# An attention block's backward tail: weights loaded in the last head group, partial sums in the drain, DMA transposes, modulation gradients off TensorE

## The chip, the core and the metric

One core of a Trainium2 chip runs the kernel as one launch. The core has five engines, each with its own instruction stream, in order: TensorE (PE in the profile, with its weight loads as PEld), VectorE (DVE), ScalarE (ACT), GpSimd (POOL) and SyncE (SP, which here only issues DMAs). Sixteen DMA engines move data between DRAM (HBM) and the on-chip memory (SBUF); TensorE writes into PSUM, eight banks of 512 f32 columns by 128 partitions. The engines wait for each other through semaphores. The metric is device time of one execution, in microseconds, as the median over runs.

## The reference

A transformer block with adaptive layer norm and its whole backward pass: n = 2048 tokens, width D = 512, H = 32 heads of 16, dense width 1792, everything bf16 in DRAM.

```python
mod = (silu(c) @ w_mod).reshape(1, 6, 1, 512)          # sa, ca, ga, sb, cb, gb
h = layernorm(x) * (1 + ca) + sa
x = x + ga * attention(h, wqkv, wo)
h = layernorm(x) * (1 + cb) + sb
out = x + gb * (relu(h @ w1 + b1) ** 2 @ w2 + b2)
# and the vjp with grad_out: dx, dwqkv, dwo, dw1, db1, dw2, db2, dc, dw_mod
```

Four of the gradients come last, since they need the gradients dq, dk and dv of all heads. dh1 = [dq dk dv] wqkv^T is a 2048 x 512 x 1536 product. From it the gradient of the first layer norm is formed and added to the residual's, which gives dx. dwqkv = h1^T [dq dk dv]. The six rows of modulation gradients (dsa, dca, dga, dsb, dcb, dgb, each a sum over the tokens) give dw_mod, an outer product of silu(c) with the rows, and dc = silu'(c) times (w_mod times the rows).

## The kernel before, in words

The forward pass comes first. `prep()` (to about 41 us) makes the statistics of the first layer norm, the modulation vectors and the first projections. Its DMAs are issued by SP through the helper `sp`, which has one line in the profile (L178). Among them are 16 DMA transposes of w_mod (`wmod_turn`), which make four of the six transposed blocks of w_mod and store them in DRAM as `wmT_st`. Forward attention runs over heads with ACT's exponentials (L567); chunks of the dense layer and stages of preparation (`later_stage`, one every fourth unit) are slipped between. Stages 30 and 31 transpose the other two blocks of w_mod; stage 25 takes reciprocals of two modulation rows.

The attention backward (about 1140 to 2380 us) goes over 8 head groups of four heads; in each over 4 blocks of 512 keys (kc), 4 blocks of 512 queries (qc) and 4 tiles of 128 queries in such a block (qi): 512 units. Four units make a block b, which has the same kc and qc. The order of every instruction is written by hand: two lists of tokens, `order_t` and `order_n`, are gone through in turn, one per block. A token stands for a score matmul (s, L1603), an exponential on ACT (e, L1609), a pair of dP products with dS = dP * E on VectorE (D, L1623, L1625), the quads for dk and dv (q: L1663, L1672, the accumulator accVK), the transposes of dS on PE (t, L1653, copied by ACT at T, L1769), and the quads for dq (d, L1690) with their output (Q: ACT L1703 and an addition on POOL L1708). Most transposes of dS are DMA transposes issued by SP (L1638, L1640). A dictionary `todo` holds work due after a given number of dP pairs: `at(j, f, ...)` puts it there; `load` issues a DMA from ACT. Finished dk, dv pieces go to DRAM as `dVKtP` (eight tiles of 128 rows by 2048 tokens, two of them stay in SBUF) and dq as `dQc` (four tiles). Before the last group ends, five of these whole tiles (512 KB each) are loaded back by SP (`load_grads`).

After the last exponential the loop runs three blocks longer to drain its pipeline. Then comes the part with names ending in J. SP loads the other gradients, the weights `wT_all` (12 blocks of 128 x 512, 1.5 MB), the last rows of dq from SBUF (L1793), tiles of x and of the incoming dx (`load_x`, L1802, L1804) and rows of modulation gradients that went through DRAM (`rows_st`, L1808). PE transposes all twelve gradient tiles, 16 transposes each (L1944), and VectorE and ACT copy them out of PSUM (L1950, L1952) for dwqkv. Then for each of the 16 token tiles:

- PE makes dh1 with 12 matmuls (L1884).
- VectorE multiplies by 1 + ca with a sum along the row (L1888), takes the product with the normalised x with another sum (L1891), scales both sums (L1894), subtracts (L1907) and adds the rest with the residual's gradient (L1909). ACT makes the normalised tile (L1877) and the correction tq (L1896).
- PE adds up the two products over the tokens with a column of ones (`row_sums`, L1903).
- Beside that PE turns rows into columns (L1849, pcolK), adds up the c gradient with the transposed w_mod (L1855, pdc) and makes the outer products of dw_mod (L1862, pwm), which ACT copies out (L1863).

Last come 12 chains of 16 matmuls for dwqkv (L1918), each copied out by ACT and VectorE (L1922, L1929, L1931) and stored by SP. Rows 0 and 1 of the modulation gradients, which need all 16 tiles, are worked off between these chains.

## Time and profile before

| what | us |
|---|---|
| median of three runs | 2525.15 |
| lowest and highest | 2521.43, 2525.73 |
| span of the profiled execution | 2517.6 |
| PE, ACT, DVE, POOL busy | 2342.5, 2302.3, 1810.1, 350.0 |
| last exponential of the backward ends | 2380.0 |
| first full dh1 matmul of the tail | 2406.7 |
| first dwqkv matmul | 2466.6 |
| last dwqkv matmul ends | 2513.8 |

The profiled execution has a span from its first to its last instruction; the time of an execution is somewhat longer than that. Columns of a window: us, then busy time (and count) of PE, PEld, DVE, ACT and POOL, then the granted clock of PE, the DMA engines' busy share (over 1 where their packets overlap) and GB/s. A group line gives line, engine, operation, output and input, shapes and count, then busy time and the mean ns of one, then the idle time before them and what ended it. A chain line gives start, duration, what. In a timeline line the bracket at the end is the idle time before it and its releaser.

### The profile page before, as it was taken

The page shows a single profiled execution, that of the slowest core. Times are in us where ns is not written, and L with a number is a line of the kernel's source. Part 1 is how long each engine was busy: PE and PEld are TensorE (multiplying, and loading weights), DVE is VectorE, ACT ScalarE, POOL GpSimd, SP SyncE. Part 2 cuts the span into 40 slices and gives each one's busy share as a digit, 9 for nine tenths or more (in the row PEclk, how much of TensorE's full clock was granted, in tenths as well). Part 3 has the DMA queues.
Part 4 walks back from the last instruction along what each step waited for, and adds up shares of the span by engine and source line. Part 5 has one row for each costly group of instructions (what it writes and reads, how often), then busy time and mean ns, then how long its engine had stood idle before and what let it go on. Part 6 is the DMA issues. An engine that isn't in the chain of part 4 may idle for free. (4 is left out here: it accounts for less than half of the span.)

```text
span 2517.6 us, 49897 instructions
## 1 busy us (share of the span) xinstructions
PE 2342.5 (93%) x19005; PEld 776.3 (31%) x19005; DVE 1810.1 (72%) x2341; ACT 2302.3 (91%) x3577; POOL 350.0 (14%) x379
## 2 busy tenths in 40 slices
PE   7899889989988999999999999999999999999999
PEld 3232223222322323442233322233323323322343
DVE  5556153454435454579999999999999999998862
ACT  7999999999989999539999999999999999999842
POOL 2000000211323142210111101111010111100100
PEclk9999999999999999999999999999999999998999
DMA  6476455367658766979999999999999999999972
GB/s 202 136 193 165 150 122 139 96 161 144 103 85 176 151 134 119 261 208 191 202 199 210 196 206 208 201 207 202 207 202 202 209 195 203 195 208 212 196 237 72
DMA packets 1220981, 447.15 MB, mean 178 GB/s; under 512 B 1096951, under 2 KB 1191607, under 8 KB 1220486
## 3 DMA queue, kind: packets, MB, share of 16 engines
q1 hardware_dynamic: 1192822, 409.11, 82.2%
q0 software_dynamic: 10944, 16.78, 4.8%
q10 hardware_dynamic: 16976, 18.07, 2.8%
q8 instruction: 149, 2.44, 0.4%
q14 instruction: 90, 0.74, 0.1%
HBM read 96.75 MB, written 73.95 MB: 68 GB/s over the span
## 5 line engine op out<-in xcount | busy, mean ns | idle before, releaser
L1625 DVE TENSOR_TENSOR dS_u<-psD_u,E_u 128x1024 bf16<-128x1024 f32 x1024 | 1186.0, 1218 | 71.6 <-PE psD_u L1623 24.0
L567 ACT ACTIVATE ET<-psST 128x1024 bf16<-128x1024 f32 x1024 | 942.0, 1260 | 27.0 <-PE psST L565 26.5
L1609 ACT ACTIVATE E_u<-psS_A 128x512 bf16<-128x512 f32 x768 | 513.1, 668 | 10.5 <-PE psS_C L1603 8.5
L1609 ACT ACTIVATE E_u<-psS_B 128x512 bf16<-128x512 f32 x768 | 505.8, 659 | 12.1 <-DMA dsT<-dS_u 3.0
L1623 PE MATMUL psD_u<-iv,ido 32*128 32x512 bf16 x2048 | 409.6, 388 | 0.0
L565 PE MATMUL psST<-qt_sb,kt_sb 32*128 32x512 bf16 x2048 | 317.8, 387 | 62.0 <-ACT ET L567 46.6
L1609 ACT ACTIVATE E_u<-psS_C 128x512 bf16<-128x512 f32 x512 | 335.4, 655 | 3.3 <-PE psS_B L1603 1.4
L1603 PE MATMUL psS_B<-ik,iq 32*128 32x512 bf16 x768 | 295.3, 385 | 12.8 <-ACT E_u L1609 5.5
L1603 PE MATMUL psS_A<-ik,iq 32*128 32x512 bf16 x768 | 293.4, 382 | 10.9 <-DVE dwlast L237 1.0
L1603 PEld LDWEIGHTS <-iq 32*128 32x128 bf16 x2048 | 130.2, 91 | 316.1 <-issue 298.8
L1663 PE MATMUL accVK<-dS_u,qz 128*32 128x512 bf16 x2048 | 213.3, 390 | 0.4 <-PE psD_u L1623 0.2
L581 PE MATMUL oacc<-ET,vaug 128*32 128x512 bf16 x2048 | 207.7, 396 | 2.2 <-DVE ostage L585 2.2
L1672 PE MATMUL accVK<-E_u,dOs_tok 128*16 128x512 bf16 x2048 | 204.1, 387 | 0.0
L1708 POOL TENSOR_TENSOR dQacc<-dQacc,dqtmp 128x512 f32<-128x512 f32 x64 | 81.2, 1268 | 852.0 <-ACT dqtmp L1703 852.0
L1603 PE MATMUL psS_C<-ik,iq 32*128 32x512 bf16 x512 | 194.7, 380 | 4.2
L565 PEld LDWEIGHTS <-kt_sb 32*128 32x128 bf16 x2048 | 85.8, 91 | 352.2 <-issue 324.6
L1690 PE MATMUL dqacc<-dsT,KS_tok 128*32 128x512 bf16 x2048 | 146.5, 384 | 18.5 <-DMA dsT<-dS_u 4.3
L1769 ACT ACTIVATE dsT<-ptT 128x1024 bf16<-128x1024 bf16 x128 | 145.8, 1139 | 7.9 <-PE ptT L1653 7.3
L251 DVE COPY part<-pm 128x512 f32<-128x512 f32 (+2 forms) x103 | 63.5, 617 | 114.8 <-PE pm L233 111.5
L1623 PEld LDWEIGHTS <-ido 32*128 32x128 bf16 x2048 | 104.6, 91 | 98.9 <-issue 92.9
L1663 PEld LDWEIGHTS <-qz 128*32 128x32 bf16 x2048 | 58.4, 94 | 177.9 <-issue 162.9
L581 PEld LDWEIGHTS <-vaug 128*32 128x32 bf16 x2048 | 53.1, 93 | 121.4 <-issue 121.4
(407 smaller groups left out, 2516.3 us busy)
## 6 DMA issues: line engine op xcount, KB each, us to landing
p_st<-part POOLq DMA_DIRECT2D x36, 256.0 KB, 5.2
kt_sb<-qkT_st SPq DMA_DIRECT2D x124, 64.0 KB
wA<-in_B_w_dram SPq DMA_DIRECT2D x28, 256.0 KB
wB<-w1T_st SPq DMA_DIRECT2D x21, 256.0 KB
wA<-w2T_st SPq DMA_DIRECT2D x21, 256.0 KB
wB<-in_B_w_dram SPq DMA_DIRECT2D x21, 256.0 KB
p_st<-part POOLq DMA_DIRECT2D x25, 192.0 KB, 5.3
p_st<-part SPq DMA_DIRECT2D x18, 256.0 KB
```

What stands on the lines that cost most here:

```text
L565: PE.matmul(ps[:, hi, :], kt_sb[r:r + 32, kt * P:(kt + 1) * P], qt_sb[r:r + 32, :], start=True, stop=True, tile_position=(r, 0))
L567: ACT.activation(ET[:, 2 * pair:2 * pair + 2, :], ps[:], AF.Exp, scale=SCALE)
L581: PE.matmul(oacc[32 * hq:32 * hq + 32, :], lhsT, ET[:, hq, :], start=(kt == 0), stop=(kt == TT - 1), tile_position=(0, 32 * hq), skip_grou ...
L1603: PE.matmul(psS[:], st["q"][r:r + 32, qt * P:(qt + 1) * P], st["k"][r:r + 32, kc * 512:kc * 512 + 512], start=True, stop=True, tile_positi ...
L1609: ACT.activation(bst[u][0][:, hq, :], sst.pop((u, hq))[:], AF.Exp, scale=SCALE)
L1623: PE.matmul(psD[:, hi, :], st["do"][r:r + 32, qt * P:(qt + 1) * P], st["v"][r:r + 32, kc * 512:kc * 512 + 512], start=True, stop=True, til ...
L1625: DVE.tensor_tensor(dS_u[:, 2 * pair:2 * pair + 2, :], psD[:], E_u[:, 2 * pair:2 * pair + 2, :], ALU.mult)
L1663: PE.matmul(cur["vk"][32 * hq:32 * hq + 32, :], hst[hg]["qz"][:, qt, hq, :], bst[u][1][:, hq, :], start=(qt == 0), stop=False, tile_positi ...
L1672: PE.matmul(acc[32 * hq:32 * hq + DH, :], dOs_tok[:, qt, (hg * 4 + hq) * DH:(hg * 4 + hq + 1) * DH], E_u[:, hq, :], start=False, stop=(qt ...
L1690: PE.matmul(acc[32 * hq:32 * hq + 32, :], KS_tok[:, kc * 4 + kt, h * DH:h * DH + 32], tT[:, :, hq * 4 + kt, :], start=(kt == 0), stop=(kt ...
L1708: POOL.tensor_tensor(dst2, dst, tmp[:], ALU.add)
L1769: ACT.activation(dst, pt[:], AF.Identity)
```

## The change

- **Prep.** `wmod_turn`, `wmod_store` and the buffer `wmT_st` are gone, as are stages 25, 30 and 31 and the buffer `rows_st`. silu(c) and its derivative are kept as columns (`siluc_f`, `dsilu`).
- **Last head group.** 32 DMAs of 128 KB, issued by ACT, one every third dP pair: 20 quarter tiles of the five gradient tiles that SP loaded whole, and the 12 blocks of the transposed weights, which go into free columns of `KS_tok` and `dOs_tok` (`w_rows`).
- **Drain.** The loop ends with its last block, and the drain is written out. Between its quads PE makes the part of dh1 whose sources are there (`early`: 6, later 7 of 12), for tiles 0 to 5, in six PSUM banks. PE turns four gradient tiles (`turn_vk`); the other eight are turned later by DMA transposes from SP (`turn_dma`).
- **Modulation rows.** They no longer go through DRAM. `factors` takes reciprocals of 128 x 512 on VectorE, `mod_row` spreads a row over the partitions with a selector matmul, `wmod_grad` scales it on ACT by a column of silu(c), and `c_grad` multiplies w_mod, loaded a second time in its own layout, by the row with a sum on VectorE.
- **Each tile.** VectorE's last addition goes to POOL (`dx_out`), the output is stored for each tile, and row sums are made four tiles at a time in the four column groups of PE (`row_sums`), added up by `sum_parts` and `sum_total`.
- **dwqkv.** The chains come in the order b = 1, 2, 0; the transpose that ends the c gradient (`c_out`) lies before the last chain.

The core of the diff:

```diff
-            def wmod_turn(j):
-                for q in range(4):
-                    sp(tmpT[:, 4 * (j % 2) + q, :], w_mod[:, (4 * j + q) * P:(4 * j + q + 1) * P], True)
-                if j > 0:
-                    wmod_store(j - 1)
-
-            def wmod_store(j):
-                sp(wmT_st[j], tmpT[:, 4 * (j % 2):4 * (j % 2) + 4, :])
-
-            for j in range(4):
-                wmod_turn(j)
-            wmod_store(3)
...
+            POOL.tensor_copy(siluc_f[:], siluc_col)
+            POOL.tensor_scalar(dsilu[:], sig_col, -1.0, 1.0, ALU.mult, ALU.add)
+            POOL.tensor_tensor(dsilu[:], dsilu[:], c_col, ALU.mult)
...
-        stages = [*range(4, 14), *range(4), 30, 31, *range(14, 26)]
+        stages = [*range(4, 14), *range(4), None, None, *range(14, 25)]
...
+        pieces = []
         for i, key in enumerate(("q", "k", "v", "do")):
+        for (key, i), dsrc in zip([("vk", 0), ("vk", 1), ("vk", 2), ("vk", 3), ("dq", 0)], (dVKtP,) * 4 + (dQc,)):
+            pieces += [(xs[key, i][r:r + 32, :], dsrc[i][r:r + 32, :]) for r in range(0, P, 32)]
+        pieces += [(w_rows(j), wT_st[j].rearrange("p (a b) -> p a b", a=2)) for j in range(12)]
+        for i, (to, fro) in enumerate(pieces):
+            at((HG - 1) * 128 + 14 + 3 * i, load, to, fro)
...
-            for b in range(NU // 4 + 3):
+            for b in range(NU // 4):
...
+            early = (("vk", 6), ("vk", 0), ("vk", 1), ("vk", 2), ("vk", 3), ("dq", 0))
+            late = (("dq", 1), ("vk", 4), ("dq", 2), ("vk", 5), ("dq", 3))
...
+            def dh1(t, srcs):
+                pd = acc_of(t)
+                for key, i in srcs:
+                    PE.matmul(pd, xs[key, i][:, t * P:(t + 1) * P], w_rows((4 if key == "vk" else 0) + i),
+                              start=(key, i) == early[0], stop=(key, i) == late[-1])
+            def turn_vk(i):
+                pt = psd.tile([P, TT, P], BF, name="ptv", tag="pd")
+                for t in range(TT):
+                    PE.transpose(pt[:, t, :], xs["vk", i][:, t * P:(t + 1) * P], identb[:])
+                for g in range(2):
+                    DVE.tensor_copy(tokA[:, i, 8 * g:8 * g + 8, :], pt[:, 8 * g:8 * g + 8, :])
...
+            load(xs["dq", 1], dQc[1])
+            load(xs["dq", 3][0:64, :], dQc[3, 0:64, :])
+            k_quad(NU - 2)
+            dp_pair(NU - 1, 1)
+            dh1(0, early)
+            v_quad(NU - 2)
+            pe_turn(B_last, 0)
+            dh1(1, early)
+            copy_turn(0)
+            load(xs["vk", 4], dVKtP[4])
+            load(xs["dq", 2], dQc[2])
+            pe_turn(B_last, 1)
+            copy_turn(1)
+            k_quad(NU - 1)
+            v_quad(NU - 1)
+            load(xs["vk", 5], dVKtP[5])
+            turn_vk(0)
+            for kt in range(4):
+                dq_quad(B_last - 1, kt)
+            dq_out(B_last - 1)
+            def last_rows(cols):
+                for h in range(4):
+                    SP.dma_start(out=xs["dq", 3][64 + DH * h:64 + DH * h + DH, cols], in_=dq_last[32 * h:32 * h + DH, cols])
+            last_rows(slice(0, 3 * 512))
...
+        def constants():
+            POOL.memset(thirty2[:], 1.0 / 32)
+            POOL.tensor_copy(selb[:], identb.rearrange("p (j c) -> p j c", c=32)[:, :, 0:1].to_broadcast([P, 4, P]))
+            POOL.tensor_copy(rowsb[0:97, :], sums[0:97, :])
+            DVE.scalar_tensor_tensor(out=nb1[:], in0=mean1[:], scalar=-1.0, in1=rstd1[:], op0=ALU.mult, op1=ALU.mult)
+        def factors():
+            DVE.tensor_scalar(nrd[:], rstd1[:], -1.0 / D, None, ALU.mult)
+            DVE.reciprocal(rec4, cb1_bc)
+            for r in (32, 64):
+                DVE.tensor_tensor(rowsb[r:r + 1, :], sums[r:r + 1, :], rec4[r:r + 1, :], ALU.mult)
+            DVE.reciprocal(rec1, ca1_bc)
+        def mod_row(k):
+            j = (5, 3, 4, 2)[k]
+            pm = psx.tile([P, 512], F32, name="pmod", tag="px")
+            PE.matmul(pm[:], selb[0:97, k, :], rowsb[0:97, :], start=True, stop=True)
+            ACT.activation(dmodb[:, j, :], pm[:], AF.Identity)
+        def wmod_grad(ic, js, k):
+            buf = dwms[:, ic % 2]
+            ACT.activation(buf[:, k, :], dmodb[:, js[k], :], AF.Identity, scale=siluc_f[:, ic:ic + 1])
...
+        def load_wmod(ic):
+            rows = w_mod[ic * P:(ic + 1) * P, :]
+            load(hsets[0][wnat[ic]][:], rows[:, 0:4 * D])
+            load(dOs_tok[:, 8 + 2 * ic:10 + 2 * ic, :], rows[:, 4 * D:6 * D].rearrange("p (j d) -> p j d", d=D))
+        def c_grad(j, ic):
+            nat = hsets[0][wnat[ic]][:, j * D:(j + 1) * D] if j < 4 else dOs_tok[:, 8 + 2 * ic + j - 4, :]
+            junk = big.tile([P, D], BF, name="junk", tag="uqa", bufs=2)
+            DVE.tensor_tensor_reduce(out=junk[:], in0=nat, in1=dmodb[:, j, :], scale=1.0, scalar=0.0,
+                                     op0=ALU.mult, op1=ALU.add, accum_out=cacc[:, ic, j:j + 1])
+        def c_out():
+            dc = big.tile([P, DC], F32, name="dcol")
+            DVE.tensor_reduce(dc[:], cacc[:], AX.X, ALU.add)
+            DVE.tensor_tensor(dc[:], dc[:], dsilu[:], ALU.mult)
+            pc = psx.tile([P, 512], F32, name="pcT", tag="px")
+            PE.transpose(pc[0:DC, 0:P], dc[:], identf[:])
+            dcb = big.tile([DC, P], BF, name="dcb")
+            ACT.activation(dcb[:], pc[0:DC, 0:P], AF.Identity)
...
+            s12 = big.tile([P, 2], F32, name="s12a", tag="s12a", bufs=2)
+            DVE.tensor_tensor_reduce(out=dxn[:], in0=pd, in1=ca1_bc, scale=1.0, scalar=0.0,
+                                     op0=ALU.mult, op1=ALU.add, accum_out=s12[:, 0:1])
...
+        def dx_out(t):
+            uq = big.tile([P, D], BF, name="uqa", tag="uqa", bufs=2)
+            DVE.scalar_tensor_tensor(out=uq[:], in0=dxs[t][0][:], scalar=rstd1[:, t:t + 1], in1=tqs.pop(t)[:], op0=ALU.mult, op1=ALU.add)
+            POOL.tensor_tensor(dx_tile(t), dx_tile(t), halves(uq[:]), ALU.add)
+            SP.dma_start(out=halves(out1_v[:, t, :]), in_=dx_tile(t))
...
+        def row_sums(g):
+            if g == 0:
+                rsums.extend(psx.tile([P, 512], F32, name="rsumJ", tag=tag) for tag in ("accVK", "px"))
+            srcs = [dxs.pop(4 * g + i) for i in range(4)]
+            for k, acc in enumerate(rsums):
+                for i in range(4):
+                    PE.matmul(acc[32 * i:32 * i + 32, :], ones_bf[:, 0:32], srcs[i][k][:], start=(g == 0), stop=(g == 3),
+                              tile_position=(0, 32 * i), skip_group_check=True)
...
+        def sum_total(k):
+            pm = psx.tile([P, 512], F32, name="ptot", tag=("accVK", "px")[k])
+            PE.matmul(pm[:], thirty2[:], totals["part"][:, k, :], start=True, stop=True)
+            DVE.tensor_tensor(dmodb[:, k, :], pm[:], rec1, ALU.mult)
...
+                ACT.activation(wblk[:, 0:256], pw[:, 0:256], AF.Identity)
+                DVE.tensor_copy(wblk[:, 256:512], pw[:, 256:512])
...
+        def turn_dma(key, i):
+            if key == "vk":
+                if not tokB:
+                    tokB["t"] = tpool.tile([P, 4, TT, P], BF, name="dvk_tokB", tag="dsT")
+                dst = tokB["t"][:, i - 4]
+            else:
+                dst = KS_tok[:, :, i * P:(i + 1) * P]
+            SP.dma_start(out=dst, in_=xs[key, i], transpose=True)
+        early7 = early + (("vk", 7),)
+        with tc.manual_schedule(engines={PE.engine, ACT.engine, DVE.engine, SP.engine, POOL.engine}):
+            for g in range(3):
+                load_x0(g)
+                load_dx(g)
+            constants()
+            turn_vk(1)
+            for g in range(3, 6):
+                load_dx(g)
+            turn_vk(2)
             norm_tile(0)
+            norm_tile(1)
+            turn_vk(3)
+            factors()
+            for t in range(2):
+                dh1(t, early7[6:])
+            for kt in range(4):
+                dq_quad(B_last, kt)
+            dq_out(B_last)
+            load_x0(3)
+            last_rows(slice(3 * 512, n))
+            for t in range(2, 6):
+                dh1(t, early7)
+                mod_row(t - 2)
             for t in range(TT):
+                dh1(t, (early7 if t >= 6 else ()) + late)
+                if t + 2 < TT:
+                    norm_tile(t + 2)
+                ln_grad(t)
...
+                wmod_grad(t // 4, (2, 3, 4, 5), t % 4)
+                if 2 <= t < 10 and t % 2 == 0:
+                    turn_dma("vk", 3 + t // 2)
+                if 5 <= t < 9:
+                    g = t - 5
+                    load(h1J[:, 4 * g:4 * g + 4, :], h1_st[:, 4 * g:4 * g + 4, :])
+                if t % 4 == 3 and t > 4:
+                    row_sums(t // 4 - 1)
+            for i in range(4):
+                load_wmod(i)
+            for i in range(4):
+                turn_dma("dq", i)
+            order = [(b, ic) for b in (1, 2, 0) for ic in range(DC)]
+            cg = [(j, ic) for j in (2, 3, 4, 5, 0, 1) for ic in range(DC)]
+            for k, (b, ic) in enumerate(order):
+                dwqkv(k, b, ic)
+                if k == 0:
+                    dx_out(TT - 1)
+                if k == 1:
+                    row_sums(3)
+                    sum_parts()
+                if k == 2:
+                    sum_total(0)
+                    sum_total(1)
+                if 3 <= k < 11:
+                    for j, i in cg[3 * (k - 3):3 * (k - 3) + 3]:
+                        c_grad(j, i)
+                if 4 <= k < 8:
+                    wmod_grad(k - 4, (0, 1), 0)
+                    wmod_grad(k - 4, (0, 1), 1)
+                if k == 10:
+                    c_out()
```

## The prediction

> **What bounds the kernel now.** I read the page, then the chain of waits of the end in order of time, the queues' timelines, then groups and windows.
>
> ```profile
> span 2517.6 us, 49897 instructions
> PE 2342.5 (93%) x19005; PEld 776.3 (31%) x19005; DVE 1810.1 (72%) x2341; ACT 2302.3 (91%) x3577; POOL 350.0 (14%) x379
> 2030.00:2180.00 150.00, 144.51 (x1394) 44.82 (x1394) 142.57 (x124) 147.58 (x283) 17.99 (x13) 0.99 1.18 196
> 2400.00:2410.00 10.00, 5.18 (x28) 3.12 (x29) 3.06 (x6) 2.43 (x3) 0.00 (x0) 0.66 0.82 210
> 2440.00:2460.00 20.00, 20.00 (x86) 6.76 (x85) 14.33 (x38) 12.85 (x21) 0.00 (x0) 1.00 0.47 161
> ```
>
> The third line is a window of the attention loop (PE, PEld, DVE, ACT, POOL busy, clock, DMA share): ACT 147.6 of 150 us, the DMA engines full. After 2400 PE is the only bound: 20.00 of 20. The last exponential ends at 2380.0. From there the chain is:
>
> ```profile
> 2389.02 8.03 DMA qz<-dQc
> 2397.07 7.60 DMA row<-rows_st
> 2406.68 6.15 PE pdh L1884 x24
> 2412.84 0.52 PE rsumJ L1903 x2
> ...
> 2466.62 3.56 PE pwq L1918 x16
> ```
>
> The reader is to see four stretches: drain and transposes to 2406.68 (26.7 us), dh1 to 2466.62 (59.94), dwqkv to its end 2513.77 (47.15), then 3.83 for eviction and store; together 137.6 = 2517.6 − 2380.0. In dh1 only 192 matmuls x 0.225 = 43.2 us are dh1 itself (12 take 2.70); 16.7 us are row sums (0.52 a tile), column turns, c gradient (pdc, 4 x 0.86) and weight-gradient outer products (pwm, 8 x 0.53).
>
> **The sum's base.** The profiled span is 2517.6; the median run is 2525.15, so 7.55 us lie around it, which I keep.
>
> **1. Prep.** SyncE (SP) loses 16 transposes and 4 stores of w_mod:
>
> ```profile
> 13.21 12.04 SPq L178 DMA_TRANSPOSE tmpT<-in_w_mod_dram  x8
> 49.33 0.95 SPq L178 DMA_DIRECT2D v_st<-vP  x2
> 55.51 1.94 ACT L567 ACTIVATE ET<-psST 128x1024 bf16<-128x1024 f32 x2 [2.97 <-PE psST L565]
> ```
>
> The stores of V (vP is ready near 41 us) queue behind them; VectorE waits for their buffer, PE for VectorE, and at 55.5 the exponentials stand 2.97 us. Afterwards forward attention is bound by ACT, so what is gained here stays. The ends are 0 (ACT's own chain covers the wait anyway) and 6 (this hole and the 3.46 us idle before the first exponential). I take 3, the hole the trace ties to that queue. The row sigmoid on ACT (0.61) is inside this bound; the deleted later stages (two 3.3 us reciprocals, eight transposes) lie under a full ACT: nothing. The POOL column operations replace 2.27 us of row operations: nothing.
>
> **2. Last head group.** Five whole loads on SP become 32 pieces of 128 KB issued by ACT, 20 for the same gradients and 12 for wT (1.5 MB more). ACT is the bound here, so each issue could hold an exponential. The row to go by: from 2100 to 2240 ACT issued 18 loads, from 2240 to 2380 four:
>
> ```profile
> L1609 ACT ACTIVATE E_u<-psS_A 128x512 bf16<-128x512 f32 x87 | 58.0, 667 | 0.0
> ...
> L1609 ACT ACTIVATE E_u<-psS_A 128x512 bf16<-128x512 f32 x84 | 56.0, 666 | 0.3 <-PE psD_u L1623 0.3
> ```
>
> The window with loads did more exponentials, 231 in all against 224. So: nothing. Bounds: a gain of 0.5 (SP's five issues go) and a loss of 32 x 0.35 us = 11 if every issue showed. The 1.5 MB at 200 GB/s is 7.5 us of DMA beside the dS transposes; if it is all late the last transpose lands that much later (rival C).
>
> **3. Drain, to the start T0 of the full dh1 tiles (before: 2406.68).** The 24x8 transposes on PE become 4x16 for vk0–3; the other eight tiles are turned by DMA later. Added: 42 of dh1's matmuls (9.5 us), four selector matmuls. In order on PE: two turns and the 12 early matmuls fit into the wait for the last dS transpose, which lands near 2389 as before; VectorE's copies of the turned tiles (two of 0.686 each) queue behind nb1, which writes where dS lay and waits for the same landing (before, L1796 stood 8.0 us). So turn 1 is copied out by 2390.6 and frees its bank; turn 2, block 126's quad (16 matmuls, 1.05), turn 3 (16 transposes, about 1.9) and block 127's quad end near 2395.2, dh1 of tile 2 (7 x 0.225) at 2396.8. Then the first selector matmul waits for factors(): two reciprocals of 128x512 on VectorE. The row for 1x512 is 3.31 us, and I take it for 128 rows too (128x128 took 0.96, so four times that is 3.8); behind the copies (end 2395.5), with two 0.67 products, that is 2400.3, a stall of 3.5 us. Behind that matmul PE holds tiles 3–5 and three selectors, 5 us: T0 = 2405.5. Bounds 2402 (stall hidden) and 2412 (landing 7 us late). The old 5.2 us hole for the rows from DRAM goes; this stall is what is late next. Gain 1.2.
>
> **4. dh1.** PE keeps 150 x 0.225 = 33.75 plus three groups of row sums at 0.65 (8 matmuls, two quads of about 0.33 as accVK's): 35.7 instead of 59.94. That uncovers VectorE. A tile costs it:
>
> ```profile
> L1888 DVE CUSTOM_DVE_ANT_0 dxn<-pdh,modbc 128x512 bf16<-128x512 f32 x16 | 11.1, 691 | 13.0 <-PE pdh L1884 13.0
> L1909 DVE SCALAR_TENSOR_TENSOR dx1J<-uqa,rstd,dx1J 128x512 bf16<-128x512 bf16 x16 | 12.0, 752 | 0.6
> ```
>
> 0.69 + 0.08 + 0.69 + 0.08 + 0.17 + 0.75 = 2.46 (the subtraction L1907, 0.42, is gone), x 16 = 39.4. But the last add moves to POOL, 1.34 a tile (L307), and both engines then read SBUF:
>
> ```profile
> 801.73 0.61 POOL L593 CAST obf<-ostage 128x512 bf16<-128x512 f32 x1 [3.19 <-DVE ostage L585]
> 802.30 1.16 POOL L170 TENSOR_TENSOR racc<-racc,g_c 128x512 f32<-128x512 f32 x1
> ...
> 802.37 1.37 DVE L331 TENSOR_TENSOR atmp<-a_c,modbc 128x512 bf16<-128x512 bf16 x1
> ```
>
> That VectorE product takes 0.426 by its median; begun under a POOL add it ends 0.28 after the add. dS_u (L1625), with one input in PSUM, never passes 1.227 us though 96 POOL adds run beside it. So behind each add the next tile's dxn (from PSUM) runs on, and prod (two SBUF inputs) is held until the add ends: 0.15 + 1.25 − 0.80, about 0.6, at most 0.95 as in the row. I take 0.55: 3.0 a tile, 48.2 in all; bounds 39.4 and 54.6. The Trainium skill (SBUF — State Buffer, "SBUF: two separate sides") states the lock whole: a VectorE instruction with two SBUF inputs and a GpSimd instruction that reads SBUF exclude each other, whoever starts second waits. By that rule alone c12 and dxn go free, as I assume; were every vector instruction held, it would be 54.6, and the rows of dS_u speak against that. ACT needs 0.80 + 0.81 + 0.80 a tile (norm, tq, and the weight gradient scaled by silu c, taken as L1877) and some 14 DMA issues at 0.35: 44, under VectorE.
>
> PE runs ahead in six banks; it waits some 1.5 us for tile 11's row sums, does two dwqkv chains (7.1) and stands for tile 15's products until T0 + 48.3. With that group's 0.65: T0 + 49.
>
> **5. dwqkv.** Ten chains remain at 3.56. sum_total behind the third needs an ACT copy that queues behind w_mod loads, which wait for the last output stores: ready near T0 + 53.3 against 52.5 on PE, 0.8; the two fp32 matmuls (0.59 each, L1255) with their waits 1.5: T0 + 55. Eight chains: 83.5. The transpose pcT before the last chain waits for the 24 c-gradient reductions (0.77 each, three per chain, hidden but the last three) with reduction and product: 3.6, bounds 0 and 6. Last chain 3.57, end 3.83: T0 + 94.5. The eight DMA transposes are SP issues of about 3 us (L1638's form, 1.7 to 4.8); those of vk end near T0 + 30 and are used at T0 + 60, those of dq end T0 + 65 to 72 behind w_mod and are used at T0 + 73: nothing taken, up to 10 at the other end (rival C). The per-tile output stores double their issues on SP, under VectorE.
>
> A 5.2 us hole on PE left the clock at 0.66 in 2400–2410 and 24 dh1 matmuls at 6.15 instead of 5.40; I count 0.75 within the 3.5 and 3.6 above, not on top.
>
> **Sum.** 2405.5 + 94.5 = 2500.0, 17.6 less; prep 3: span 2497.0, time 2504.5 us, 0.8% faster.
>
> **The rivals.** A is this forecast, 2498 to 2510, with all terms near where I put them.
>
> B, covers hold: T0 2402 (3.5), POOL's adds hold nothing (3.2: without them T0 + 91.3, since PE then stands 2.5 at sum_total instead of 5.5 and 0.8 earlier), pcT free (3.6), two waits of 2 less, prep 6 (3 more): 2504.5 − 15.3 = 2489. For it: VectorE was busy 14 of 20 us, ACT 13. Against: L331's row.
>
> C, transfers bind: the drain 2412 (6.5 more), dq's turns late by 5: 2516. For it: DMA share 1.18 in the loop, one SP queue for stores and transposes, ACT issues that wait for landings in order. Against: the share falls to 0.47 by 2440.
>
> D, slower: a piece issued by ACT in the last head group waits for an older landing and every exponential waits behind it. The point where it decides is 20.6 us, or 0.65 per piece over 32. At 1 us each: 2504.5 + 32 = 2536. For it: the DMAs are full there. Against: the 231 and 224 above.
>
> E, the transposes out of prep free nothing: A + 3 = 2507.5, inside A.
>
> **How the numbers follow.** A (with E) 0.45, B 0.15, C 0.24, D 0.12, a mixture that ends within 0.2% (5 us, about what a measurement of this kernel tells from no change) 0.04. Faster 0.84, same 0.04, slower 0.12. The range goes from B's end, 2491, to past C, 2521, and leaves out D and B's edge. A's own is 2498 to 2510.
>
> **What would show it.** Right: ET's hole at 55 us gone; the last exponential within 1 us of 3 us earlier; selector matmuls waiting for VectorE near 2397; prod (now after POOL adds) at 1.2 us instead of 0.69; PE standing before the last row sums; pcT waiting for VectorE. Wrong: exponentials with idle put down to ACT's queue in the last head group; dwqkv's last four chains waiting for a DMA transpose.

## The result, and the profile after

The changed kernel takes 2546.02 us (median of 4 runs, 2537.7 to 2547.74) against 2523.29 us (2517.16 to 2525.73) for the kernel before on the same chip: ratio 1.0097, 95% interval 1.0073 to 1.012. It is 1% slower; 0.8% faster was forecast, and the time lies outside the forecast range.

The profiled execution is the quickest of the four: 2537.7 us for a span of 2535.7. The page's span and busy times of the changed kernel, then the same windows as before (us, PE, PEld, DVE, ACT, POOL busy, granted clock, DMA share, GB/s) and one in the w_qkv chains:

```profile
span 2535.7 us, 49562 instructions
PE 2329.2 (92%) x18810; PEld 770.2 (30%) x18810; DVE 1816.2 (72%) x2364; ACT 2299.1 (91%) x3574; POOL 369.5 (15%) x401
```

```profile
2030.00:2180.00 150.00, 144.71 (x1375) 45.44 (x1378) 141.33 (x124) 146.67 (x279) 16.71 (x12) 0.98 1.18 204
2400.00:2410.00 10.00, 7.24 (x69) 4.32 (x70) 5.77 (x11) 2.53 (x4) 2.58 (x4) 0.62 0.38 102
2440.00:2460.00 20.00, 17.04 (x84) 7.28 (x83) 15.25 (x34) 13.39 (x20) 6.92 (x6) 1.00 1.15 251
```

PE has 13 us less to do over the span, as planned, and the span is 18 us longer. Where PE was busy for 20.00 of 20 us, from 2440 to 2460, it now stands for 3, with the DMA share up from 0.47 to 1.15. PE is no longer what binds this stretch; whether it is the transfers themselves or the order in which they are asked for, a share does not say.

The chain that ended last, in order of time (start, duration, what), with its long pieces after the loop:

```profile
2379.80 10.21 SPq L1616
2390.10 10.98 DMA dsT<-dS_u
...
2409.47 3.27 DVE iqs L1872
2414.83 2.99 PE pdh L1777 x7
...
2472.80 7.06 DMA out_dram<-dwms
2482.20 5.57 PE pwq L1984 x16
...
2526.89 5.15 PE pwx L1984 x16
```

The last transposed dS is on the way until 2401.1 where it landed near 2389 before; a reciprocal follows; and a w_qkv chain starts at 2482.2 only, after a landing on which ScalarE stood.

I cut each profile at the same marks. The loop runs from the first to the last exponential of the backward; the drain from there to VectorE's first product of dh1 with 1 + ca; dh1 to the end of its last such product; w_qkv to the end of its last matmul. The last head group is the loop's last 256 exponentials and is counted in the loop. Each row is one profiled execution. "Before again" is a second profile of the kernel before; the other rows are experiments of the next section.

| us | first backward exp. | loop | of it last head group | drain | dh1 | w_qkv | end | span |
|---|---|---|---|---|---|---|---|---|
| before | 1125.3 | 1255.2 | 161.4 | 29.9 | 56.4 | 46.9 | 3.8 | 2517.6 |
| before again | 1124.4 | 1254.9 | 156.8 | 29.6 | 56.4 | 46.9 | 3.8 | 2516.1 |
| after | 1115.2 | 1263.1 | 167.1 | 44.4 | 46.5 | 62.8 | 3.7 | 2535.7 |
| x1, drain loads on SP | 1116.3 | 1262.0 | 166.9 | 33.2 | 45.8 | 63.1 | 3.6 | 2524.1 |
| x2, w_mod loads later | 1118.5 | 1264.0 | 165.4 | 47.3 | 44.7 | 61.3 | 3.7 | 2539.6 |
| x3, prep's turns back | 1120.2 | 1269.7 | 168.8 | 48.7 | 45.4 | 64.2 | 4.0 | 2552.1 |
| x6, add on VectorE | 1118.9 | 1277.2 | 170.1 | 44.5 | 50.4 | 62.9 | 3.7 | 2557.5 |
| y2, w_mod by GpSimd | 1120.2 | 1271.0 | 169.1 | 52.9 | 48.7 | 61.3 | 3.6 | 2557.7 |
| y3, drain reordered | 1115.6 | 1267.8 | 164.7 | 44.4 | 44.4 | 63.5 | 3.6 | 2539.4 |
| y4, four edits | 1115.6 | 1254.2 | 163.1 | 37.0 | 43.9 | 57.8 | 4.2 | 2512.9 |
| w1, pieces later | 1118.4 | 1268.9 | 165.8 | 49.8 | 44.5 | 62.1 | 3.6 | 2547.2 |
| w2, before + prep's part | 1130.1 | 1255.1 | 158.3 | 29.2 | 56.4 | 46.9 | 3.8 | 2521.5 |
| w3, joined | 1113.8 | 1256.8 | 160.9 | 28.0 | 43.7 | 47.7 | 4.1 | 2494.1 |
| v1, stores by GpSimd | 1120.1 | 1269.8 | 171.6 | 43.7 | 46.1 | 63.0 | 3.7 | 2546.2 |
| v2, stores and w_mod | 1120.4 | 1260.4 | 167.5 | 49.9 | 44.4 | 52.3 | 3.7 | 2531.2 |

From before to after: the forward gained 10.1, dh1 gained 9.9, and the loop lost 7.9, the drain 14.5, w_qkv 15.9. With 0.1 at the end that is 18.2, against 18.1 between the spans. Two losses, drain and w_qkv, are larger than everything that was won.

### The profile page after: what moved, and what is told of

Its sections match the earlier page's. It is cut to its first block, busy times and chain, and to the rows that moved or that the text cites. A ratio compares the mean times of both kernels' runs of the same rounds, so it can differ in the third digit from the quotient of the medians.

```text
span 2535.7 us, 49562 instructions
## 1 busy us (share of the span) xinstructions
PE 2329.2 (92%) x18810; PEld 770.2 (30%) x18810; DVE 1816.2 (72%) x2364; ACT 2299.1 (91%) x3574; POOL 369.5 (15%) x401
## 4 chain that ended last, share of the span: by engine, by line
ACT 39%; PE 36%; issue 8%; DVE 7%; DMA 6%; SPq 1%; ACTq 1%; POOL 0%; DVEq 0%; POOLq 0%
ACT E_u L1585 23%; ACT ET L567 12%; PE dqacc L1666 4%; PE psST L565 3%; DMA dsT<-dS_u 3%; PE pm L233 3%; PE psS_A L1579 3%; PE accVK L1639 2%; ACT dsT L1751 2%; PE oacc L581 2%; PE psS_B L1579 2%; PE pm L400 2%; PE pm L414 2%; PE psS_C L1579 2%; PE pm L489 1%
## 5 line engine op out<-in xcount | busy, mean ns | idle before, releaser
L251 DVE COPY part<-pm 128x512 f32<-128x512 f32 (+2 forms) x103 | 63.5, 616 | 113.8 <-PE pm L233 107.6
L1639 PEld LDWEIGHTS <-qz 128*32 128x32 bf16 x2048 | 58.5, 94 | 178.0 <-issue 163.1
L585 DVE COPY ostage<-oacc 128x512 f32<-128x512 f32 x32 | 22.0, 689 | 97.0 <-PE oacc L581 80.7
```

Of the source, the lines that this page charges most:

```text
L1639: PE.matmul(cur["vk"][32 * hq:32 * hq + 32, :], hst[hg]["qz"][:, qt, hq, :], bst[u][1][:, hq, :], start=(qt == 0), stop=False, tile_positi ...
```

## The experiments

### x1, x2, x3, x6: one suspect each

**x1_drain_sp.** The five gradient loads (four whole tiles and a half) that ScalarE asks for while the last dS transposes are on the way are issued by SP instead, which puts them behind those transposes.

```diff
-            load(xs["dq", 1], dQc[1])
+            SP.dma_start(out=xs["dq", 1], in_=dQc[1])
```

(and the same for the other four)

> Edit: the five loads of gradients in the drain are issued by SP, behind its last transposes of dS, instead of by ACT beside them; all else as in the changed kernel. Theory A, these 2.3 MB take the DMA engines from the last dS transposes (11.5 us at 200 GB/s): the last four transpose issues take about 18 us again instead of 32, the last landing comes near 2389 instead of 2401, and the time falls by 8 to 12 us, to about 2536. Rival B, the 32 pieces of the last head group have left a backlog that delays the transposes: the landing stays within 3 us of 2401 and the time within 3 us of the changed kernel's 2546.

Measured: 2531.99 us (10 runs), ratio to before 1.0052 (1.0034 to 1.007). The median is 13.5 us above that of the kernel before on the same chip, where the changed kernel's is 22.7 above; the drain falls from 44.4 to 33.2 us. SP's timeline over the last transposes, in the kernel before, then the changed one, then x1:

```profile
2368.33 15.37 SPq L1640 DMA_TRANSPOSE dsT<-dS_u  x3
2383.76 3.11 SPq L1638 DMA_TRANSPOSE dsT<-dS_u  x1
```

```profile
2367.16 22.85 SPq L1616 DMA_TRANSPOSE dsT<-dS_u  x3
2390.10 8.99 SPq L1614 DMA_TRANSPOSE dsT<-dS_u  x1
```

```profile
2364.82 19.42 SPq L1616 DMA_TRANSPOSE dsT<-dS_u  x3
2384.33 4.15 SPq L1614 DMA_TRANSPOSE dsT<-dS_u  x1
```

The fourth issue ends 6.4 us after the loop's last exponential before, 20.8 us after it in the changed kernel, 10.2 us after it in x1. In the changed kernel ScalarE issues the five loads (2.3 MB) from 2377.25 to 2383.9, into the middle of that. So plain loads that run beside DMA transposes stretch them, and those of the drain did it here. The other profiles agree: in all nine kernels with these loads on ScalarE the last two transposes issue in 8.9 to 16.2 and 4.2 to 13.0 us, and the fourth issue ends 20.5 to 28.9 us after the last exponential; in the six without, 4.8 to 4.9, 3.0 to 4.2 and 6.4 to 10.2 us. What x1 has left over before goes with the loads of x0 and dx that ScalarE issues in both kernels ahead of the last exponential (seven from 2359 to 2373 in the changed one): with those out of the way too, in y4 and w3 below, the fourth issue ends 8.6 and 7.9 us after it.

**x2_wmod_later.** ScalarE asks for w_mod two chains later, behind the row sums.

```diff
-            for i in range(4):
-                load_wmod(i)
             for i in range(4):
                 turn_dma("dq", i)
...
                     sum_parts()
+                    for i in range(4):
+                        load_wmod(i)
```

> Edit: the eight loads of w_mod, issued by ACT, stand behind the second dwqkv chain and the copy of the row sums instead of ahead of the first chain's eviction. Theory A, ACT stands at these issues for landings of output stores, the eviction behind them is late, and PE's second chain waits for it: the 9.3 us wait of the second chain goes, its cold 5.57 us becomes 3.6, and the time falls by 8 to 11 us, to about 2536. Rival B, the wait only moves: w_mod is then late for the c gradient and the transpose before the last chain waits longer; the time falls by less than 4 us.

Measured: 2546.69 us (4 runs), ratio 1.0101 (1.0059 to 1.0143), no gain; w_qkv 61.3 against 62.8. The wait moved from the second chain to the sixth. In the chains of x2, ScalarE waits for a w_mod load with the copy of a block, and the next chain that shares the PSUM tile waits for it (engine, tile, line, what it waited for: us, times, longest):

```profile
ACT wqblk L1996 <- DMA dOs_tok<-in_w_mod_dram: 15.8, 1, 15.8
...
PE pwq L1984 <- DVE wqblk L1998: 9.6, 2, 8.7
```

The edit was at the right place; that it would free the chain was wrong. What ScalarE stands for can be read from its timeline in the changed kernel, together with the semaphore numbers that the trace keeps:

```profile
2471.89 0.37 ACTq L1561 DMA_DIRECT2D dOs_tok<-in_w_mod_dram  x1
2478.61 0.34 ACTq L1561 DMA_DIRECT2D iq<-in_w_mod_dram  x1
...
2481.30 0.38 ACT L1996 ACTIVATE wqblk<-pwq 128x256 bf16<-128x256 f32 x1 [9.53 <-issue]
```

The DMAs of SP and ScalarE tell of their landing through the same eight semaphores, used over and over, and 298 of ScalarE's 313 issues in this profile wait for the semaphore that they will themselves raise, that is, for the landing of the transfer that had it before, whoever issued that one. The load at 2478.61 has number 110; a store of dx by SP had it before and landed at 2478.59. In x2 the fourth load of w_mod stands until a dq transpose of SP has landed at 2495.16. GpSimd's DMAs have eight semaphores of their own (111 to 118).

**x3_prep_back.** The 16 transposes and 4 stores of w_mod go back into the prep; nothing reads them.

```diff
+            for j in range(4):
+                wmod_turn(j)
+            wmod_store(3)
             stats_tiles(0, range(4))
```

> Edit: the 16 transposes of w_mod and their four stores are put back into prep, where nothing uses them; the later stages stay removed. Theory A, each hole of the forward exponentials has its own cause and only the one at 55 us comes from prep: the first backward exponential is 3 to 4 us later than the changed kernel's 1115, and the time rises by about 3 us, to 2549. Rival B, prep's queue sets all of the 10 us that the forward pass gained: the first backward exponential comes near 1125 and the time rises by 7 to 10 us.

Measured: 2550.92 us (4 runs), ratio 1.0108 (1.0059 to 1.0156). The first backward exponential starts at 1120.2 rather than 1115.2, and I first took these 5 us for the prep's share. The other profiles overrule that: the 11 kernels with the changed forward and without these transposes show 1113.8 to 1120.4, and the forward's first exponential starts at 41.5 here against 41.8 in the changed kernel and 41.4 in the kernel before. x3 lies inside the scatter; no price of the prep's transposes can be read from it. The hole of 2.97 us at 55 us, which the forecast tied to them, is absent from x3, and also from the second profile of the kernel before (z0), though both have the transposes.

**x6_add_on_vector.** The last add of a tile goes from GpSimd back to VectorE.

```diff
-            POOL.tensor_tensor(dx_tile(t), dx_tile(t), halves(uq[:]), ALU.add)
+            DVE.tensor_tensor(dx_tile(t), dx_tile(t), halves(uq[:]), ALU.add)
```

> Edit: the addition of the residual's gradient goes back from POOL to VectorE. Theory A, POOL's addition holds a vector instruction with two inputs in SBUF: the product behind it falls from 1.14 us to 0.69, a tile on VectorE costs 2.46 + 0.42 = 2.88 us against 2.70, and the time stays within 4 us. Rival B, the product is long for another reason: it stays at 1.14, a tile costs 3.1 and the dh1 stage grows by 6 us.

Groups of the dh1 stretch, of the changed kernel, then of x6 (busy, mean ns of one | idle before):

```profile
L1939 POOL TENSOR_TENSOR dOs_tok<-dOs_tok,uqa 128x512 bf16<-128x512 bf16 x15 | 17.3, 1153 | 43.3 <-DVE uqa L1938 41.8 <-DMA dvk_tokB<-qz 1.6
L1928 DVE CUSTOM_DVE_ANT_0 prod<-dxn,xn1b 128x512 bf16<-128x512 bf16 x16 | 16.4, 1025 | 0.8
```

```profile
L1928 DVE CUSTOM_DVE_ANT_0 prod<-dxn,xn1b 128x512 bf16<-128x512 bf16 x16 | 11.1, 692 | 0.8
...
L1939 DVE TENSOR_TENSOR dOs_tok<-dOs_tok,uqa 128x512 bf16<-128x512 bf16 x15 | 6.4, 425 | 0.5
```

The product with two SBUF inputs takes 0.692 us without GpSimd's add. With the add on GpSimd it takes 1.14 us in 12 of the 16 tiles, behind an add, and 0.69 in the other four; 1.025 is the mean. So the lock is real, and where it holds it costs 0.45 us, about what the add costs on VectorE itself (0.425). A tile that waits for nothing takes 2.71 us in the changed kernel and 2.72 in x6: the add's place does not matter there. That dh1 is 50.4 us against 46.5 comes from two waits: from one tile to the next it is once 8.01 and once 6.06 us in x6, 5.40 and 4.86 in the changed kernel. The first of them lies behind a load of h1 on ScalarE, which waits for the semaphore of a DMA transpose of SP. The single time, 2559.39 us, is no measure of the edit: 14 us of it are a longer loop, before the edit's place.

### y2, y3, y4: the other waits, and all at once

**z0_before_again** is the unchanged kernel before, profiled a second time; its row is in the table.

> The kernel before, unchanged, for a second profile. Question: from the first to the last backward exponential the first profile of it shows 1254.5 us, five profiles of kernels with the changed tail 1262 to 1276, though the instructions of the first seven head groups are the same. Theory A, the loop differs from execution to execution in either kernel: anything from 1250 to 1270. Rival B, the loop of the changed kernel is longer by itself: 1252 to 1257 again.

It took 2517.87 us: the cut points of the tail agree with the first profile to 0.3 us per stretch, the last head group to 5 us. The loop takes 1254.9 us again, as rival B had it.

**y2_wmod_pool.** GpSimd, not ScalarE, issues the w_mod loads.

```diff
-            load(hsets[0][wnat[ic]][:], rows[:, 0:4 * D])
+            POOL.dma_start(out=hsets[0][wnat[ic]][:], in_=rows[:, 0:4 * D])
```

(and the second half likewise)

> Edit: the eight loads of w_mod are issued by POOL instead of ACT, at the same place. Theory A, what costs is that an engine with evictions behind it stands at an issue until older transfers land: the 9.3 us wait of the second dwqkv chain goes and none takes its place; from the first full dh1 tile to the end 104 us instead of 114, time 8 to 11 us lower, about 2536. Rival B, the transfers themselves come too late, whoever issues them: the c gradient or the DMA transposes make the chains wait, and the time falls by less than 4 us.

Measured: 2557.23 us (4 runs), ratio 1.0161 (1.0136 to 1.0187); w_qkv 61.3. The wait at the second chain is gone, and another has come, in the chains of y2:

```profile
ACT wqblk L1996 <- DMA out_dram<-wqblk: 13.7, 1, 13.7
...
PE pwq L1984 <- DVE wqblk L1998: 9.5, 2, 8.6
```

The blocks have three buffers, and their stores are queued on SP behind the four dq transposes. The chain that waits is again the sixth. The theory's first half came out, its "none takes its place" did not. The rest of the loss lies ahead of the edit (loop 1271.0, drain 52.9), and why it is larger than in the changed kernel is not known.

**y3_drain_order.** The column `nb1` gets its own tile and is made early, all four turns and both reciprocals come ahead of the last quads, and the loads of x0 and dx behind them.

```diff
             turn_vk(0)
+            turn_vk(1)
+            DVE.reciprocal(rec4, cb1_bc)
+            turn_vk(2)
+            turn_vk(3)
+            DVE.reciprocal(rec1, ca1_bc)
             for kt in range(4):
                 dq_quad(B_last - 1, kt)
```

> Edit: nb1 gets memory of its own and is made before the drain; all four PE turns and both reciprocals stand ahead of the last dq quads; the loads of x and of the residual gradient stand behind the last quads. The drain's loads are still ACT's. Theory A, VectorE's copies queue behind nb1, which waits for the last dS transpose, and PE stands 18 us for these copies: the first full dh1 tile starts about 11 us after the last landing instead of 20, and the time falls by 8 to 10 us, to about 2537. Rival B, what follows the landing (quads, last rows, loads) sets the start anyway: less than 3 us.

Measured: 2543.78 us (4 runs), ratio 1.0112 (1.0076 to 1.0148), no better than the changed kernel's 1.0097; drain 44.4 as there: order on PE and VectorE does not matter while the last transposed dS is late.

**y4_all.** x1, y2 and y3 together, the h1 loads by GpSimd and the pcT transpose behind the last chain.

```diff
-                if k == 10:
+                if k == 11:
                     c_out()
```

> Edit: the drain's loads by SP as before, the drain's order as in the run above, the loads of w_mod and of h1 by POOL, and the transpose that ends the c gradient behind the last dwqkv chain. Theory A, the parts add up: 13 us for the drain's loads, 9 for the order, 9 for w_mod, 5 for the transpose with its cold chain, some 3 for h1: about 2507, below the kernel before (2518). Rival B, they cover each other, since the tail's transfers bind: 2520 or more.

Measured: 2528.19 us (10 runs, 2514.7 to 2543.32), ratio 1.0046 (1.002 to 1.0072). The 2507 of the theory was missed, and the median lies on the rival's side. The profile is of the quickest run. The drain is 37.0, longer than in x1: the x0 and dx loads, now all ahead of the first normalised tile on ScalarE, hold it for 12.2 us; they stand for rows of dq that SP loads (`iq<-dQst`), whose semaphores they take over. The chains of y4 wait for the stores, as in y2:

```profile
ACT wqblk L2003 <- DMA out_dram<-wqblk: 14.9, 2, 14.1
```

### w1, w2, w3: the loop, the prep, a faster kernel

**w1_pieces_later.** The 32 pieces of the last head group start 16 units later.

```diff
-            at((HG - 1) * 128 + 14 + 3 * i, load, to, fro)
+            at((HG - 1) * 128 + 30 + 3 * i, load, to, fro)
```

> The changed kernel with one number altered: the 32 load pieces of the last head group start at its unit 30 rather than at its unit 14 (still every third unit). Counted by exponentials, the last head group takes 167.1 us in the changed kernel, 166.9 in the one with the drain loads on SP, 161.4 and 156.8 in the two profiles of the kernel before; the other seven groups agree. ScalarE's idle time in that group has two lumps, 4.5 us around 2240 and 4.1 us around 2370. Theory: the first lump is made by the pieces that ScalarE issues between its dQc stores at 2232.9 to 2240.2: with them out of the way the third store is issued as soon as its data is there, the lump falls from 4.5 to under 1.2 us, the last head group to 161 to 164 us and the time by 3 to 5 us, to about 2542. Rival: the third dQc store waits for transposes that are as late without the pieces; the lump stays at 4 us or more and the time moves by less than 1 us. A second lump, at 2370, should stay in both cases, since the x0 and dx loads that are issued from 2359 on are not moved.

What it was aimed at, in ScalarE's timeline of the changed kernel:

```profile
2235.56 0.48 ACTq L1561 DMA_DIRECT2D iq<-dVKtP  x1
...
2239.71 0.34 ACTq L1561 DMA_DIRECT2D dQc<-dQst  x1
2240.09 0.60 ACT L1585 ACTIVATE E_u<-psS_C 128x512 bf16<-128x512 f32 x1 [3.17 <-DMA dsT<-dS_u]
```

After a piece, the store of dq stands until 2239.71 and the exponentials behind it for 3.17 us. It waits for semaphore 110, which a dS transpose of SP had before it. In w1 that lump of idle time falls from 4.5 to 1.2 us, as the theory said, and 2.4 us come up near 2310; the last head group takes 165.8 us where 161 to 164 was expected, the time is 2541.58 us (4 runs, 2529.68 to 2557.39; ratio 1.01, 1.0059 to 1.0142), not to be told from the changed kernel. The group's own lengths say more than one run: with pieces at their place and the x0 and dx loads in the group, 165.4 to 171.6 us in eight kernels (mean 168.3); with the pieces later 165.8; with the x0 and dx loads behind the quads 164.7 and 163.1 (y3, y4); with both (w3) 160.9; in the kernel before and w2 161.4, 156.8 and 158.3 (mean 158.8). So the loads that the change puts there cost some 9.5 us, by means over profiles that differ by up to 6 us among themselves.

**w2_before_prep.** The kernel before with the prep's part alone: its 16 transposes of w_mod become later stages of the forward.

```diff
-            for j in range(4):
-                wmod_turn(j)
-            wmod_store(3)
...
-        stages = [*range(4, 14), *range(4), 30, 31, *range(14, 26)]
+        stages = [*range(4, 14), *range(4), 30, 31, *range(14, 30)]
```

> The kernel before with one part of the change alone: the 16 transposes of w_mod and their 4 stores leave the prep and become four more of the later stages of the forward loop (the stages at units 58 and 62 stay). Theory: the prep's part of the change is worth what the restored-prep run showed with the other sign, 5.0 us, and does nothing to the loop: first backward exponential 1120 us (1125.3 before), loop 1252 to 1258 us, time 4 to 6 us below the kernel before on the same chip. Rival one: the four new stages make new holes of about the sizes seen at the old ones (2.97, 3.11, 1.77 us), so that little or nothing of the 5 us is left at the first backward exponential. Rival two: a lighter prep goes with a slower backward loop, which would explain the longer loop of the changed kernel by the prep's change: loop 1261 us or more and no gain in the time.

Measured: 2525.47 us (12 runs) against 2519.17, ratio 1.0031 (1.0014 to 1.0047): slower. Rival one holds, in one place. SP's and PE's timelines of w2:

```profile
280.23 8.31 SPq L178 DMA_TRANSPOSE tmpT<-in_w_mod_dram  x4
...
289.20 0.57 SPq L178 DMA_DIRECT2D qt_sb<-m_st  x1
```

```profile
291.11 0.74 PE L565 MATMUL psST<-qt_sb,kt_sb 32*128 32x512 bf16 x4 [8.36 <-DMA qt_sb<-m_st]
```

A query block's load sits behind four transposes on SP, PE stands for 8.4 us, and the exponentials with it for 7.5. The kernel before has the same at stage 30, in the same two timelines:

```profile
154.19 5.53 SPq L178 DMA_TRANSPOSE tmpT<-in_w_mod_dram  x4
...
162.79 0.55 SPq L178 DMA_DIRECT2D qt_sb<-m_st  x1
```

```profile
164.97 0.53 PE L565 MATMUL psST<-qt_sb,kt_sb 32*128 32x512 bf16 x4 [3.73 <-DMA qt_sb<-m_st]
```

The exponentials stand for 3.8 to 4.8 us there in all three profiles with stage 30 and in none without it. Stage 30, which the change deletes together with its neighbour 31, had this price; for the transposes in the prep no profile but the first shows one.

**w3_joined.** y4 with the pieces from unit 30, the x0 and dx loads of the drain by GpSimd, the first tile's ahead, and the output blocks of the key and value parts stored by GpSimd.

```diff
-                SP.dma_start(out=dst, in_=wblk.rearrange("p (v c) -> p v c", v=2))
+                POOL.dma_start(out=dst, in_=wblk.rearrange("p (v c) -> p v c", v=2))
...
-                load(x0_tile(t), halves(x_dram[:, t, :]))
+                (POOL if g < 4 else ACT).dma_start(out=x0_tile(t), in_=halves(x_dram[:, t, :]))
```

> The kernel with the drain loads on SP, the drain in the other order, GpSimd's w_mod and h1 loads and the late pcT, plus four edits at the waits that its profile showed: the pieces from unit 30 on, the x0 and dx loads of the drain issued by GpSimd with the first tile's ahead, the w_qkv output blocks of the key and value parts stored by GpSimd rather than by SP behind the four dq transposes. Its quickest profile had a span of 2512.9 us. Theory (waits in issue order): 4 us at the dQc stores, 6 of the 12.25 us that the first normalized tile waited, and 10 to 12 of the 14.1 us that ScalarE waited for a stored output block go: span 2489 to 2497 us, median of the runs 2493 to 2508, faster than before by 0.5 to 1%. Rival (the transfers themselves bind: some 5 MB behind the last head group): the first normalized tile and the output blocks wait as long for other transfers, and the span stays at 2508 us or more.

Measured: 2501.81 us (6 runs, 2496.33 to 2509.29), ratio 0.994 (0.9917 to 0.9963): faster than the kernel before, by 0.6%. Span (2494.1) and median lie where the theory put them. Of its parts, the wait for the first normalised tile fell as expected, from 12.2 to 6.6 us; the one for a stored block fell by less than 10 to 12 (14.9 to 7.2 us in all, the longest from 14.1 to 7.2), and the last head group by 2 rather than 4 (163.1 to 160.9). The chain of w3, its long pieces between 2380 and 2470:

```profile
2386.76 4.03 DMA KS_tok<-in_A_x_dram
...
2429.29 9.45 DMA out_dram<-dwms
2446.10 3.63 PE pwq L1991 x16
2450.79 10.62 DMA out_dram<-wqblk
2464.58 3.61 PE pwq L1991 x16
```

A 10.6 us landing of an output block is still on it, worth 2.1 us of PE's time; the whole tail is 123.5 us against 137.1 before and 157.4 after.

### v1, v2: one queue or two in the w_qkv stretch

**v1_stores** has the stores' line of w3 alone:

```diff
-                SP.dma_start(out=dst, in_=wblk.rearrange("p (v c) -> p v c", v=2))
+                POOL.dma_start(out=dst, in_=wblk.rearrange("p (v c) -> p v c", v=2))
```

**v2_both** has that and y2's edit:

```diff
-            load(hsets[0][wnat[ic]][:], rows[:, 0:4 * D])
+            POOL.dma_start(out=hsets[0][wnat[ic]][:], in_=rows[:, 0:4 * D])
```

> The changed kernel with the w_qkv output blocks of the key and value parts stored by GpSimd rather than by SP; the w_mod loads stay on ScalarE. Theory (two queues in series): the wait of 9.3 us at the second chain is ScalarE standing at its w_mod loads and stays at 8 us or more, so the stretch of the w_qkv chains stays at 59 to 63 us (62.8 in the changed kernel). Rival (the stores on SP are the cause): the wait shrinks below 4 us and the stretch falls to 50 to 56 us.

> The changed kernel with both edits: w_mod loads issued by GpSimd and the output blocks of the key and value parts stored by GpSimd. Theory (two queues in series): neither wait is left, and the stretch of the w_qkv chains falls from 62.8 us to 49 to 54 (the 3.7 us of the pcT wait and the cold chain behind it stay). Rival (the transfers themselves bind): a wait of 7 us or more appears at another chain, and the stretch stays at 58 us or more, as with the w_mod loads alone (61.3).

Measured: v1 2548.62 us (2 runs), ratio 1.0139 (1.0104 to 1.0175), v2 2532.56 us (4 runs), ratio 1.006 (1.0017 to 1.0103); w_qkv 63.0 and 52.3 us, where the changed kernel has 62.8 and the w_mod loads alone gave 61.3. In v1 the second chain waits 9.66 us. Second chain of the changed kernel and of v2, from PE's timeline (v2's row shows 12 of the 16 matmuls, those inside the queried window):

```profile
2482.20 5.57 PE L1984 MATMUL pwq<-dvk_tokA,h1J 128*128 128x512 bf16 x16 [9.26 <-DVE wqblk L1998]
```

```profile
2479.47 2.75 PE L1984 MATMUL pwq<-dvk_tokA,h1J 128*128 128x512 bf16 x12 [0.93 <-DVE wqblk L1998]
```

Either edit alone gives 1.5 us or nothing, both give 10.5. Two queues held the chains one behind the other, which was the theory: ScalarE stood at its loads, and SP held the stores. GpSimd issues both on semaphores of its own. The Trainium skill (DMA: Bandwidth & Descriptors, "Rules for kernel authors") has it that spreading DMAs over the issuing engines saves issue time only, since the same 16 engines move them. The trace agrees in that what goes is time at the issue, for which ScalarE and the stores stood, but that time was 10.5 us of the kernel's. What is left of 52.3 over w3's 47.7 is the pcT transpose, which waits in both the changed kernel and v2 as below, with a chain behind it that takes 5.30 us rather than 3.62, since PE's granted clock is lower there (0.57 from 2526.6 to 2530.5):

```profile
2526.62 0.27 PE L1908 MATMUL pcT<-identf,dcol 128*4 128x128 f32 x1 [3.22 <-DVE dcol L1906]
2526.72 5.30 PE L1984 MATMUL pwx<-KS_tok,h1J 128*128 128x512 bf16 x16
```

## Why the prediction was wrong

**The base.** I kept 7.55 us around the span, the difference between one span and the median of other runs. Runs of the kernel before with a span of their own show 1.7 to 1.9. The profiled execution of before was a run of about 2519.4 us, so some 5.7 us of the 2504.5 were no part of the sum. This made the forecast less wrong, not more. The last exponential of before ends at 2380.5; 2380.0 is the end of the one on the chain.

**1, prep: 3 us.** Right in the total's sign, wrong in the place. The first backward exponential came 10.1 us earlier in this profile and 7.3 on average over the kernels with this forward (1117.5 over 11 without the prep's turns, 1124.9 over two of before). The 3 us rested on the hole at 55 us, which is missing from the second profile of the same kernel: one profile was not enough to tie it to a queue. The prep's transposes showed no price in x3, and moving them cost time in w2. The step that failed is "the deleted later stages ... lie under a full ACT: nothing": stage 30's transposes held a query load on SP, and with it the exponentials, for 3.8 to 4.8 us. The rest of the 7.3 is not settled; holes of 2 to 7 us near 730 us come and go between profiles of one forward.

**2, last head group: nothing.** Failed: it costs some 9.5 us (158.8 to 168.3). I priced ScalarE's issues by their count in two windows, which is rival D's form; a piece's issue in the changed kernel did cost only its 0.31 to 0.53 us. What cost was a store that stood after a piece for the landing of a dS transpose, and the x0 and dx loads, which are issued before the last exponential, beside the transposes that PE waits for. My part on the drain did not place those loads at all. Rival D was right on the side of the result and in its mechanism, an issue that waits for an older landing with the exponentials behind it (the idle time put down to it was one of the forecast's own signs of being wrong), and wrong on the price: 9.5 us, not 20.6 or more.

**3, drain: a gain of 1.2.** Failed at "the last dS transpose, which lands near 2389 as before". It landed at 2401.1, because the same section's loads were moved from SP, behind the transposes, to ScalarE, beside them; I had listed a landing 7 us late only as a bound, for another reason. Everything behind waits as I said, only 12 us later. VectorE's timeline of the changed kernel:

```profile
2401.31 0.18 DVE L1868 SCALAR_TENSOR_TENSOR nb<-mean,rstd 128x16 f32<-128x16 f32 x1 [21.53 <-DMA dsT<-dS_u]
2401.42 2.48 DVE L1787 COPY dvk_tokA<-ptv 128x1024 bf16<-128x1024 bf16 x4
...
2409.39 3.35 DVE L1872 RECIPROCAL iqs<-modbc 128x512 f32<-128x512 bf16 x1
```

nb1 and the copies wait for that landing; the reciprocal of 128 rows takes 3.35 us as read from the row of 1 x 512 (3.31). From the landing to the first full dh1 tiles (2421.4) it is 20.3 us against the 16.5 forecast: PE waits for each turn's copy and for the selector (3.3), and its next dh1 matmuls start 0.426 us apart instead of 0.215.

**4, dh1: VectorE at 3.0 us a tile, 48.2.** Right in the mechanism; that 46.5 lies so near is in part luck. The parts of a tile are 0.684 + 1.025 + 0.228 + 0.747 = 2.68 us by their means, and a tile that waits for nothing takes 2.71, not 3.0; waits that the forecast did not have, up to 2.7 us for a tile, make up for most of the difference. The lock behind GpSimd's add was taken at 0.55 us and is 0.45 where it holds; the Trainium skill (SBUF — State Buffer, "SBUF: two separate sides") has a VectorE instruction with two SBUF inputs and a GpSimd instruction that reads SBUF exclude each other, and the rows of x6 agree: only the product with two SBUF inputs got shorter, the one with its input in PSUM stayed at 0.684 and 0.685. Rival B's price for no lock at all (2.46 a tile) does not come out.

**5, w_qkv.** Failed at "an ACT copy that queues behind w_mod loads ... 0.8". The mechanism was right and its size was off by a factor of ten: ScalarE stood 9.5 us at those loads, and PE 9.3 at the second chain. I also charged it to the wrong instruction. Not the copy of the row sums but that of the first output block stood there, and the second chain has its accumulator in the same PSUM tile, so PE stood with it. "Dq's transposes on SP: nothing taken" was right for dq (no chain waited for them) and wrong for what is queued behind them, the stores of the blocks. With the pcT wait at 3.2 (3.6 forecast) and a chain of 5.3 behind it, 1.7 longer than the others, where I had counted 0.75 within the 3.6, the stretch from the start of the full dh1 tiles to the end was 114.3 us, not 94.5.

**The rivals.** C came nearest: it named the queue on SP, transfers that bind, and ScalarE's issues that wait for landings. It priced them at 11.5 us in all; against the forecast's own terms the loss was 17.6 us in the drain (43.1 from the last exponential to the full dh1 tiles, not 25.5) and 19.8 behind it (114.3, not 94.5). The forecast's own sum was not unreachable: with the queues apart, w3's tail of 123.5 us comes near the 120.0 of the forecast (2500.0 − 2380.0).

**What stays open.** Of the 7.9 us that the loop lost, the last head group explains 5.7 in this pair of profiles and all by the means. The first seven groups take 1091 to 1107 us in the changed kernels (mean 1098.7) and 1093.8 to 1098.1 in three profiles of before's loop (mean 1096.2); why x6, y2, y3 and w1 take 1102.0 to 1107.2 us there, 6 to 11 above the mean of the other eight (1096.1), was not tried. Why a plain load slows a DMA transpose beside it is not shown either, only that it does.

## What to carry to other kernels

When loads change their queue, place each one on the new queue and ask both what it runs beside and what stands behind it: in this kernel a DMA transpose beside plain loads took longer, and a load, a store or a copy behind a waiting issue took the wait over. Look up which semaphore an issue waits for: with eight of them shared by SP and ScalarE, a load on one engine stood for a transfer of the other that it had nothing to do with. A wait that is held by two queues in turn gives nothing back when one of them is cleared, so look for the next releaser before an edit is called useless. Sparing PE in the tail paid here only when the transfers were asked for in an order that did not hold the other engines (w3).

## What was not expected of the hardware

- Loads beside DMA transposes: three transposes issued on SP took 15.37 us in the kernel before, 19.42 with the x0 and dx loads beside them (x1), 22.85 with the drain's 2.3 MB as well; the last one landed 12 us later.
- ScalarE stood 9.5 us among the issues of its w_mod loads, for the landing of SP's stores that had had their semaphores; GpSimd issued the same loads at some 0.55 us each without standing (v2, y4, w3), on semaphores 111 to 118, which SP and ScalarE do not use, and in v2 PE's wait went with it.
- Runs of one kernel go with the granted clock: over 17 runs of the kernel before, those under 2512 us had 0.986, those over 2524 us 0.980 to 0.982. The times differ by up to 16 us, as much as most edits here are worth, so a single time of a kernel like this says little where its profile's stretches say much. Whether the clock makes the time or longer waits of PE lower the clock was not separated.
